# Attention beside a state-space scan on one core: another order ahead of the first exp, and a new plan

## The chip, the cores and the metric

The kernel runs on one core of a Trainium2 chip. Its time is the device time of one execution in microseconds (us); of several executions the median counts, and lower is better. Five engines work side by side, each through its own queue in order: TensorE (PE; PEld is its weight load), VectorE (DVE), ScalarE (ACT), GpSimd (POOL) and SyncE (SP), which issues most of the DMAs. They meet through semaphores.

## What is computed

Two independent layers on sequences of 2048 rows of 640 bf16 numbers; their outputs are laid side by side.

```python
# A: a diagonal state space layer
Lam_bar = jnp.exp(dt * Lam);  B_bar = ((Lam_bar - 1.0) / Lam)[:, None] * Bmat
Bu = jnp.einsum("bld,pd->blp", x + 0j, B_bar)
for t in range(L): h = Lam_bar[None, :] * h + Bu[:, t, :]
y = 2.0 * jnp.einsum("blp,dp->bld", hseq, Cmat).real + x * Dskip
# B: attention, 32 query heads of 20 numbers, one key head and one value head
q = (x @ wq).reshape(B, S, 32, 20);  k = x @ wk;  v = x @ wv
p = softmax(einsum("bhqd,bkd->bhqk", q, k) * 20 ** -0.5)
o = einsum("bhqk,bkd->bhqd", p, v) ... @ wo
```

## The kernel before

Softmax dominates: 2048 tiles of 128 keys by 512 queries need an exponential. The kernel takes no exact row maximum but a bound: the key maximum times the sum of a query's absolute values. That bound enters as one more row of the queries (QT), so scores come out of TensorE ready for the exponential.

Tiles go two ways. ScalarE reads two or three of them at once out of a **slot** (two slots SC0 and SC1 of three PSUM banks each) and writes bf16 weights PR. VectorE takes other tiles, mostly from the third bank of a slot, and makes an approximate exponential by writing the bits of a bf16 number; it and GpSimd then add constants to make three shifted copies in BIG, and TensorE sums all four with scaled values VS. A fill of a slot with scores is one step on TensorE, since scores use 32 of its 128 rows each; a piece of other work, such as a query product, may **ride** on the free rows. Everything else, the scan of layer A, query products and output products, is fitted between.

The order of all of this is no loop. The program hands steps (`pe`, `dve`, `act`, `pool`, `dma`) with estimated durations, dependencies and priorities to a planner (`Schedule`) that plays them through; `Emitter` writes each engine's queue in the order found and puts in the semaphore waits. Seeds (`SEEDS`) shift the background work, and the table `STAGES` gives the planner's weights from a given tile count on. `LANDS` and `XB` say when it expects the first loads. None of these numbers are in the program that runs, only the order that they lead to.

What comes ahead of the first exp:

- `loads`: x for layer B comes in four blocks of 512 rows. Blocks 0 and 1 are loaded plain (xn, into CT) and turned by TensorE against an identity (L730, `turn`), then copied out (L1139 on VectorE, L1142 on ScalarE); blocks 2 and 3 come by transposing DMA (L715). The key weights wk are spread four times over the columns (`wks_op`, L1047, on ScalarE). The first 80 columns of wq (`wqa`) are padded by GpSimd (L1069) for the first query product.
- `kv_steps`: per block five products make the keys, spread over four groups of partitions (L1162); VectorE reduces their absolute maximum (L1168, into mab); the keys are scaled into KT on ScalarE (L1174) or VectorE (by the helper `ts`, L867), as `KEYS` says. Values (L1218) follow and are copied to VP (L1226) and, scaled, to VS.
- `bound`: one reduction over the five maxima (L1194) and the mask times the result, M0 (L866).
- `qt_task`: the first query product (L1279) goes to QT on ScalarE (L1292), its absolute values (L866) are multiplied by M0 on TensorE (L730, four matmuls 32x512), and VectorE writes the final QT (L867).
- `ssm_scalars`: the scan's tables `tab` by sine on ScalarE from the angles `fr`, of which VectorE makes five and GpSimd (L2215) five more.
- TensorE runs products of zeros (L730 MATMUL MB<-PR) where it would idle here.
- `attention`: when all six banks of the slots are free (`mine`), fills (L1626) and exps (L1530) begin. The third bank of each slot is lent to background work until the first query load is ordered.

Names that are not tensors: `prio` orders steps that could start at the same time (lower first), `gate` holds a step back in the plan, `port` marks the SBUF port that VectorE and GpSimd share. L800, L810 and L730 are helpers of TensorE, L862, L866 and L867 of VectorE, L710, L711 and L715 of loads.

Of the kernel before, what the change touches and what calls it, by code (L numbers as in the profile page):

```python
# [11 lines left out]
ACT = mybir.ActivationFunctionType  # L12
ALU = mybir.AluOpType
# [454 lines left out]
class Build:  # L468
# [79 lines left out]
    SEEDS, REPLAYS = (169732,), 12  # L548
# [321 lines left out]
    def program(self):  # L870
        self.lay_banks()
        self.firsts, self.row_mm, self.stage_dma, self.buf_user, self.unit_due = [], {}, {}, {}, {}
        self.tile_n = 0
# [156 lines left out]
    def loads(self):  # L1030
# [24 lines left out]
        self.vec_op.append(vec[3]("sp"))  # L1055
        self.wqa_op = L(wqd[:, :, 0:80], wqv[:, :, 0:80], 200000, "wqa", strided=True, writes=["wqa"], prio=0)
# [31 lines left out]
    PLAIN, KP, QR, FRP, SINP, SKIP_P, KEY_BANKS = 2, (1.04, 1.04, 1.06, 1.08), 1.05, 0.34, 0.32, 1.03, "2543016"  # L1088
    WKP, QUAD_KEYS, WKE = 0.9, 0, "a"
    TURNED, KEYS = ("adada", "adada"), "adaa"  # L1090
    XB = ((2, 0, 5, 11250.0), (3, 0, 3, 12500.0), (3, 3, 5, 13400.0))
    LANDS = (2250.0, 2400.0, 2750.0, 8200.0, 5600.0, 7900.0, 6500.0, 8450.0, 14600.0, 17000.0)
# [35 lines left out]
    def kv_steps(self):  # L1128
# [20 lines left out]
        def kv(tb):  # L1149
# [4 lines left out]
            steps = [(0, c, 512) for c in range(NC)] if tb < 3 else self.KEY_STEPS  # L1154
            for x, c, n in steps:
                at = 512 * tb + n * x
# [10 lines left out]
                if c == NC - 1:  # L1167
                    red = self.dve(lambda e, src=bank.cols(n * x, n * x + n), to=p.mab[:, tb + x:tb + x + 1]: e.tensor_reduce(  # L1168
                        out=to, in_=src, axis=AX.X, op=ALU.max, apply_absolute_value=True), 115 + 1.05 * n, deps=[prev], reads=[bank.key],
                        writes=[f"mab{tb + x}"], prio=0.31 if tb < 3 or x else 0.315)  # L1170
                    self.red_op[tb + x] = red
# [20 lines left out]
        def bound():  # L1192
            yield lambda: len(self.red_op) == 5
            m = self.dve(lambda e: e.tensor_reduce(out=p.mab[:, 5:6], in_=p.mab[:, 0:5], axis=AX.X, op=ALU.max), 120,  # L1194
                         deps=list(self.red_op.values()), reads=[f"mab{i}" for i in range(5)], writes=["mabs"], prio=0.3)
            self.m0_op = self.dve(self.ts(p.M0[:], p.mask0[:], p.mab[:, 5:6], None, ALU.mult), 200, port=True,
                                  deps=[m, self.c_op["mask0"]], reads=["mabs", "mask0"], writes=["M0"], prio=0.3)
# [529 lines left out]
    SCARCE = 8  # L1727
# [945 lines left out]
```

## Time and profile before

| | us |
|---|---|
| median of 3 executions (697.73 to 699.15) | 698.69 |
| the profiled execution, its own time | 697.62 |
| its span, first to last instruction | 695.9 |
| busy in the span: PE, ACT, DVE, POOL | 683.2, 681.8, 637.0, 470.4 |
| first exp starts | 18.41 |
| last exp ends | 687.68 |

Two engines are busy for 98% of the span, so busy shares tell little here. The granted TensorE clock is 1.00 throughout. What is of use is the view by stages (ahead of the first exp, the exps, the end), the pace of the exps in the timeline, and the chain of waits of the first stage. Note that ScalarE's entries overlap: an exp's time in the groups is longer than the distance from its start to the next one's.

### The profile page before, as it was taken

What the parts mean: (1) busy time and instruction counts of PE and PEld (TensorE: products, weight loads), DVE (VectorE), ACT (ScalarE), POOL (GpSimd) and SP (SyncE); (2) the same over time, 40 slices, a digit from 0 to 9 for tenths busy, and PEclk for the clock granted to TensorE, in tenths of its full rate; (3) what the DMA queues carried; (4) which work ended last, traced back from release to release, by engine and by line L of the source; (5) the groups of instructions that cost most, each with busy time, mean ns of one, the idle gap of its engine ahead of it and who ended that gap; (6) DMA issues with size and microseconds to landing.
All of it is one profiled execution on the core that took longest, in us unless ns stands there. A gap on an engine that the chain in (4) does not pass through costs nothing.

```text
span 695.9 us, 27390 instructions
## 1 busy us (share of the span) xinstructions
PE 683.2 (98%) x11488; PEld 250.6 (36%) x11490; DVE 637.0 (92%) x1243; ACT 681.8 (98%) x703; POOL 470.4 (68%) x796
## 2 busy tenths in 40 slices
PE   8999999999999999999999999999999999999998
PEld 5322332334334333333433333334333332343335
DVE  7899999999999889999999999999999999977795
ACT  7999999999999999999999999999999999999996
POOL 4256666564587668767778777676776767788880
DMA  9659641211130111102110101131000001110001
GB/s 217 175 127 187 139 103 39 62 26 32 30 94 13 32 27 27 35 21 29 44 26 22 28 27 28 35 58 20 13 15 12 20 15 36 37 29 22 21 15 41
DMA packets 77591, 34.48 MB, mean 50 GB/s; under 512 B 58350, under 2 KB 77470, under 8 KB 77470
## 3 DMA queue, kind: packets, MB, share of 16 engines
q1 hardware_dynamic: 76650, 32.57, 20.3%
q8 instruction: 92, 1.51, 0.9%
q10 hardware_dynamic: 820, 0.16, 0.1%
q14 instruction: 29, 0.24, 0.1%
HBM read 11.53 MB, written 9.75 MB: 31 GB/s over the span
## 4 chain that ended last, share of the span: by engine, by line
PE 56%; ACT 42%; DVE 1%; issue 0%
ACT PR L1530 41%; PE MB L1946 21%; PE MB L800 14%; PE SC L1626 10%; PE MB L810 8%; PE MB L730 1%; DVE BIG L867 1%; PE SC L1162 1%; PE SC L726 1%; PE MB L726 0%; ACT L2197 0%; PE SC L730 0%; DVE pvsb L1925 0%; PE MB L1279 0%; DVE QT L867 0%
## 5 line engine op out<-in xcount | busy, mean ns | idle before, releaser
L1530 ACT ACTIVATE PR<-SC 128x1024 bf16<-128x1024 f32 (+1 forms) x678 | 666.6, 1131 | 4.5 <-PE SC L1626 3.3
L1858 POOL INT64_ADD BIG<-BIG x761 | 458.1, 617 | 198.1 <-DVE BIG L867 54.7
L867 DVE TENSOR_SCALAR BIG<-SC 128x512 int16<-128x512 f32 x560 | 376.2, 684 | 38.7 <-PE SC L1626 33.1
L1946 PE MATMUL MB<-BIG,VS 128*32 128x512 bf16 (+1 forms) x2468 | 269.8, 376 | 1.2 <-DVE pvsb L1925 0.9
L1626 PE MATMUL SC<-QT,KT 32*128 32x512 bf16 (+1 forms) x2073 | 265.3, 378 | 4.4 <-ACT PR L1530 1.8
L1946 PE MATMUL MB<-PR,VP 128*32 128x512 bf16 (+1 forms) x1495 | 222.3, 378 | 0.1
L1626 PEld LDWEIGHTS SC<-QT,KT 32*128 32x128 bf16 x2073 | 67.3, 91 | 133.8 <-ACT PR L1530 77.1
L1946 PEld LDWEIGHTS MB<-BIG,VS 128*32 128x32 bf16 x2468 | 68.5, 95 | 65.5 <-issue 41.4
L1946 PEld LDWEIGHTS MB<-PR,VP 128*32 128x32 bf16 x1495 | 55.1, 94 | 45.8 <-issue 33.0
L867 DVE TENSOR_SCALAR BIG<-BIG 128x1024 int16<-128x1024 int16 (+1 forms) x136 | 52.3, 419 | 0.9 <-PE MB L1946 0.4
L800 PE MATMUL MB<-CA,W 128*32 128x320 bf16 (+2 forms) x992 | 51.4, 299 | 0.4 <-DVE BIG L2366 0.4
L810 PE MATMUL MB<-xaT,BT 32*128 32x256 bf16 x192 | 37.1, 273 | 0.0
L800 PE MATMUL MB<-CT,W 128*32 128x512 bf16 (+1 forms) x640 | 36.0, 302 | 0.6 <-issue 0.6
L800 PE MATMUL MB<-xaT,BA 128*32 128x256 bf16 x800 | 31.8, 275 | 0.0
L810 PE MATMUL MB<-diagD,xaT 32*128 32x128 bf16 x320 | 31.3, 217 | 0.0
L810 PEld LDWEIGHTS MB<-diagD,xaT 32*128 32x128 bf16 x320 | 17.7, 92 | 29.1 <-ACT PR L1530 17.7
L800 PEld LDWEIGHTS MB<-CA,W 128*32 128x32 bf16 x992 | 22.8, 96 | 14.2 <-issue 5.7
L800 PE MATMUL MB<-xaT,BT 128*32 128x256 bf16 x608 | 26.2, 274 | 0.0
L2133 DVE CAST stg<-MB 128x512 bf16<-128x512 f32 x35 | 23.8, 680 | 1.8 <-PE MB L800 1.1
L862 DVE TENSOR_TENSOR prod<-MB,tab 128x1024 bf16<-128x1024 f32 x20 | 24.3, 1215 | 0.2
L867 DVE TENSOR_SCALAR BIG<-MB 128x512 int16<-128x512 f32 x35 | 23.8, 679 | 0.6 <-PE MB L1626 0.6
L2406 DVE TENSOR_TENSOR_SCAN g<-sc,hst,prod 128x256 bf16<-128x256 f32 x30 | 22.5, 749 | 0.0
(178 smaller groups left out, 502.4 us busy)
## 6 DMA issues: line engine op xcount, KB each, us to landing
out_dram<-stg SPq DMA_DIRECT2D x33, 128.0 KB, 2.0
qd<-BIG SPq DMA_DIRECT2D x20, 128.0 KB, 2.1
QT<-qd SPq DMA_DIRECT2D x28, 80.0 KB
OP<-pvsb SPq DMA_DIRECT2D x105, 20.0 KB
rdP<-recs SPq DMA_DIRECT2D x105, 20.0 KB
lbd<-BA SPq DMA_DIRECT2D x5, 320.0 KB, 2.7
CT<-in_B_x_dram SPq DMA_DIRECT2D x2, 640.0 KB, 5.3
BA<-in_A_B_re_dram SPq DMA_DIRECT2D x1, 800.0 KB, 7.5
```

Source lines behind the costliest of these rows:

```text
L726: r = e.matmul(out[32 * j:32 * j + 32], lhsT=lhsT[:, 32 * j:32 * j + 32], rhs=rhs, start=start, stop=stop, tile_position=(0, 32 * j), skip ...
L730: return lambda e: e.matmul(out, lhsT=lhsT, rhs=rhs, start=start, stop=stop, **kw)
L800: x = e.matmul(out[32 * j:32 * j + 32], lhsT=lhsT[:, 32 * j:32 * j + 32], rhs=rhs, start=start, stop=r.end is tag, tile_position=(0, 32 * ...
L810: return lambda e: e.matmul(out, lhsT=lhsT[at], rhs=rhs[at], start=start, stop=r.end is tag, tile_position=(32 * row, 0), skip_group_check ...
L862: return lambda e: e.tensor_tensor(out, a, b, op)
L867: return lambda e: e.tensor_scalar(out, a, s1, s2, op0=op0, op1=op1)
L1530: ex = self.act(lambda e: e.activation(dst, t[:, 0:512 * n], ACT.Exp, scale=1.0 / UNIT), 0.8333 * 512 * n + 64, table="exp", deps=[op], re ...
L1626: r = e.matmul(out[:, bank.off + lo:bank.off + lo + n], lhsT=p.KT[32 * j:32 * j + 32, 128 * c:128 * c + 128], rhs=p.QT[32 * j:32 * j + 32, ...
L1858: op.fns.append(lambda e: e.int64_add(words(dst), words(src), add))
L1946: r = e.matmul(bank.tensor[32 * j:32 * j + 32, bank.off + at:bank.off + at + n], lhsT=v[:, c, 0:32], rhs=rhs[:, lo:lo + n], start=first an ...
L2133: ev = self.dve(lambda e: e.tensor_copy(st, bank.ap), 645, deps=[prev], reads=[bank.key], writes=[key], prio=self.EV, gate=(lambda: last.e ...
L2406: o = self.dve(lambda e, ri=ri, init=init: e.tensor_tensor_scan(p.g[:, u, ri, :], rdec, p.prod[:, 1, 0, ri, :], init, ALU.mult, ALU.add), ...
```

## The change

Ahead of the first exp:

1. VectorE spreads the key weights, and is to do so early (`prio=0.2`); GpSimd's angles wait for it in the plan.
2. The first wq columns and the Dskip row are issued from ScalarE's queue.
3. The keys of block 1 are scaled on VectorE, not ScalarE.
4. Block 3's keys are made in five products of 512, no longer in halves, and reduced once. The key maximum comes in two steps: the maximum of blocks 0 to 2 times the mask on ScalarE, and then, on VectorE, one instruction that takes in block 3's. The value for all blocks that the rest needs is reduced behind it.
5. The first fill waits for two banks of each slot only, so not for those of the values.

In the attention: a fill may leave out its third bank, and the wait for VectorE's reading of it, when the plan sees that reading come too late (`third_late`); such a fill holds two tiles. And the planner has another seed, other weights and other expected landings, so the order changes everywhere.

```diff
-    SEEDS, REPLAYS = (169732,), 12
+    SEEDS, REPLAYS = (696354,), 12
...
             self.wks_op = self.dve(lambda e: e.tensor_copy(spread, again), 400, deps=[self.wk_op], reads=["wkr"], writes=["wks"],
-                                   prio=0.34, port=True)
+                                   prio=0.2, port=True)
...
-        self.vec_op.append(vec[3]("sp"))
-        self.wqa_op = L(wqd[:, :, 0:80], wqv[:, :, 0:80], 200000, "wqa", strided=True, writes=["wqa"], prio=0)
+        self.wqa_op = L(wqd[:, :, 0:80], wqv[:, :, 0:80], 200000, "wqa", eng="act", strided=True, writes=["wqa"], prio=0)
+        self.vec_op.append(vec[3]("act"))
...
-    WKP, QUAD_KEYS, WKE = 0.9, 0, "a"
-    TURNED, KEYS = ("adada", "adada"), "adaa"
+    WKP, QUAD_KEYS, WKE = 0.9, 0, "d"
+    TURNED, KEYS = ("adada", "adada"), "ddaa"
...
-            steps = [(0, c, 512) for c in range(NC)] if tb < 3 else self.KEY_STEPS
-            for x, c, n in steps:
-                at = 512 * tb + n * x
+            x, n, at = 0, 512, 512 * tb
+            for c in range(NC):
...
-            yield lambda: len(self.red_op) == 5
-            m = self.dve(lambda e: e.tensor_reduce(out=p.mab[:, 5:6], in_=p.mab[:, 0:5], axis=AX.X, op=ALU.max), 120,
-                         deps=list(self.red_op.values()), reads=[f"mab{i}" for i in range(5)], writes=["mabs"], prio=0.3)
-            self.m0_op = self.dve(self.ts(p.M0[:], p.mask0[:], p.mab[:, 5:6], None, ALU.mult), 200, port=True,
-                                  deps=[m, self.c_op["mask0"]], reads=["mabs", "mask0"], writes=["M0"], prio=0.3)
+            yield lambda: all(i in self.red_op for i in range(3))
+            m = self.dve(lambda e: e.tensor_reduce(out=p.mab[:, 4:5], in_=p.mab[:, 0:3], axis=AX.X, op=ALU.max), 120,
+                         deps=[self.red_op[i] for i in range(3)], reads=[f"mab{i}" for i in range(3)], writes=["mab4"], prio=0.3)
+            m = self.act(lambda e: e.activation(p.M0[:].rearrange("p a b -> p (a b)"), p.mask0[:].rearrange("p a b -> p (a b)"), ACT.Copy,
+                                                scale=p.mab[:, 4:5]), 260,
+                         deps=[m, self.c_op["mask0"]], reads=["mab4", "mask0"], writes=["M0"], prio=0.25)
+            yield lambda: 3 in self.red_op
+            self.m0_op = self.dve(lambda e: e.scalar_tensor_tensor(out=p.M0[:], in0=p.mask0[:], scalar=p.mab[:, 3:4], in1=p.M0[:],
+                                                                   op0=ALU.mult, op1=ALU.min), 250, port=True,
+                                  deps=[m, self.red_op[3]], reads=["mab3", "mask0", "M0"], writes=["M0"], prio=0.3)
...
-        mine = [b for _, bs in self.slots for b in bs]
+        mine = [b for _, bs in self.slots for b in bs[:-1]]
...
-            yield lambda: (fill is None or fill.start is not None) and all(o.start is not None
-                                                                          for o in self.slot_last[i])
+            yield lambda: (fill is None or fill.start is not None) and all(o.start is not None for o in self.slot_last[i] if o is not self.third[i]) \
+                and self.third_known(i)
...
-            deps = list(self.slot_last[i])
+            self.skip[i] = self.third_late(i)
+            deps = [o for o in self.slot_last[i] if o is not self.third[i] or not self.skip[i]]
...
     STAGES = (
         (0, {'STAY': 1.2, 'PAUSE': 500.0, 'pe': 192.807, 'dve': 150.0, 'KEEP_C': 3, 'OPEN': 1, 'PATIENCE': 2500.0, 'MARGIN':
-            648.138, 'WAITING': 2, 'REFILL': 905.623, 'SPARE': 148.045, 'LAG': 162.255, 'SOON': 3981.867, 'EARLIER': 3, 'LATER':
...
+            569.99, 'WAITING': 3, 'REFILL': 905.623, 'SPARE': 148.045, 'LAG': 162.255, 'SOON': 224.375, 'EARLIER': 3, 'LATER': 3,
...
+    def third_late(self, i):
+
+        o = self.third[i]
+        return o is not None and (o.start is None or self.s.seen(o, "pe") > max(self.third_limit(i), self.s.t))
...
+        if self.skip[i]:
+            n, third = min(n, 2), self.third[i]
+            self.n_skip += 1
```

What this does to the queues, at three places. SP's queue, from its first loads on; in the old order:

```order
L711 DMA vrow<-in_A_Lambda_re_dram 5x128
L711 DMA CT<-in_B_x_dram 128x4x640 x2
L711 DMA vrow<-in_A_Dskip_dram 5x128
L710 DMA BIG<-in_B_wq_dram 128x5x80
L715 DMA_TRANSPOSE BIG<-in_B_x_dram 128x5x512
L715 DMA_TRANSPOSE BIG<-in_B_x_dram 128x3x512
```

and in the new one:

```order
L711 DMA vrow<-in_A_Lambda_re_dram 5x128
L711 DMA CT<-in_B_x_dram 128x4x640 x2
L715 DMA_TRANSPOSE BIG<-in_B_x_dram 128x5x512
L715 DMA_TRANSPOSE BIG<-in_B_x_dram 128x3x512
L715 DMA_TRANSPOSE BIG<-in_B_x_dram 128x2x512
```

The Dskip row and the 80 columns of wq are gone from it; they stand behind wk in ScalarE's queue, ahead of its first table load.

VectorE's queue from the last maximum but one to QT (mab are the maxima; MB2 is the bank of the first query product), in the old order:

```order
L1168 TENSOR_REDUCE mab<-SC0 128x1
L866 TENSOR_SCALAR BIG<-QT 128x512
L1168 TENSOR_REDUCE mab<-SC1 128x1 x2
L1194 TENSOR_REDUCE mab<-mab 128x1
L866 TENSOR_SCALAR M0<-mask0,mab 128x128
L867 TENSOR_SCALAR QT<-MB2,lift 128x512
```

and in the new one, from one row earlier:

```order
L866 TENSOR_SCALAR BIG<-QT 128x512
L1167 TENSOR_REDUCE mab<-SC0 128x1
L985 MEMSET VS 128x16
L1193 TENSOR_REDUCE mab<-mab 128x1
L1167 TENSOR_REDUCE mab<-SC1 128x1
L1199 SCALAR_TENSOR_TENSOR M0<-mask0,mab,M0 128x128
L1202 TENSOR_REDUCE mab<-mab 128x1
L867 TENSOR_SCALAR QT<-MB2,lift 128x512
```

Behind the last block's reduction there stands one instruction where there were two, and a reduction over few numbers has moved ahead of it.

TensorE's queue from the last keys to the first fill (SC1 is the slot in which block 3's keys and the values are made, wvr are the value weights, the bracket names what a row waits for), in the old order:

```order
L1162 MATMUL SC1<-BIG,wks 128x256 x3
L730 MATMUL MB3<-PR 128x512
L1218 MATMUL SC1<-wvr,BIG 128x20 [waits dma_wv]
L1218 MATMUL SC1<-wvr,BIG 128x20 x19
L730 MATMUL MB3<-PR 128x512 x2
L730 MATMUL MB2<-BIG,M0 32x512 [waits prog_dve]
L730 MATMUL MB2<-BIG,M0 32x512 x3
L1218 MATMUL SC1<-wvr,BIG 128x20 [waits prog_act]
L1218 MATMUL SC1<-wvr,BIG 128x20 x19
L730 MATMUL MB3<-PR 128x512 x2
L810 MATMUL SC0<-BIG 128x512 [waits dma_wq,prog_act,prog_dve]
L1626 MATMUL SC0<-QT,KT 128x512 x2
```

and in the new one:

```order
L1161 MATMUL SC1<-BIG,wks 128x512 [waits dma_xb33]
L1161 MATMUL SC1<-BIG,wks 128x512
L1224 MATMUL SC1<-wvr,BIG 128x20 [waits dma_wv,prog_dve]
L1224 MATMUL SC1<-wvr,BIG 128x20 x39
L730 MATMUL MB3<-PR 128x512
L730 MATMUL MB2<-BIG,M0 32x512 [waits prog_dve]
L730 MATMUL MB2<-BIG,M0 32x512 x3
L730 MATMUL MB3<-PR 128x512 x4
L810 MATMUL SC0<-BIG 128x512 [waits dma_wq,prog_act,prog_dve]
L1661 MATMUL SC0<-QT,KT 128x512 x2
```

The values of two blocks now stand together ahead of the product with M0; the first fill has a rider (L810) that waits for the load of wq, as before.

More of the change, by code (lines that the diff above doesn't have):

```diff
@@ L1307, in qt_task @@
         self.give(bank)
-    m0_op = None
+    m0_op = q_first = None
     row_mm = {}
@@ L1408, in attention @@
             self.misc.append(lent)
-            self.free_banks.append(lent)
+            if not lent.busy:
+                self.free_banks.append(lent)
         s.spawn(self.reclaim())
@@ new lines, in third_limit, with third_known @@
+    def third_limit(self, i):
+        ex, other = self.slot_last[i][0], self.slot_last[1 - i][0]
+        return ex.start + ex.dur + (other.dur if other.eng == "act" else 0.0) - 522.0 + self.SKIP
+    def third_known(self, i):
+        o = self.third[i]
+        if o is None or o.start is not None:
+            return True
+        at = self.third_limit(i) - 755.0
+        if self.s.t < at:
+            self.s.at(at)
+            return False
+        return True
+    def third_late(self, i):
+        o = self.third[i]
+        return o is not None and (o.start is None or self.s.seen(o, "pe") > max(self.third_limit(i), self.s.t))
@@ L1539, in fill @@
         ex.hook = on_start
-        self.slot_last[i] = [ex] + first
+        self.slot_last[i] = [ex] + first + ([third] if third is not None else [])
+        self.third[i] = first[0] if first else third
         for (b, kc, j, rhs), key in zip(ents, keys):
@@ L1815 @@
     BACKLOG = 9
-    LAST = 12
-    POOL_LAST = 14
+    LAST = 14
+    POOL_LAST = 27
     def pool_source(self):
```

77 lines of the change are left out of this document (41 added, 36 removed).

## The prediction, made before the changed kernel had run

> **What bounds the kernel now.** I read the stages first: busy time of each engine before the first exp, between the first exp's start and the last one's end, and behind it.
>
> ```profile
> core 0: us, PE busy (x) PEld busy (x) DVE busy (x) ACT busy (x) POOL busy (x), PEclk, DMA share, GB/s
> 0.00:18.41 18.41, 16.02 (x134) 9.09 (x136) 13.83 (x56) 13.03 (x21) 8.14 (x27) 1.00 0.92 225
> 18.41:687.68 669.27, 661.87 (x11232) 238.45 (x11234) 621.28 (x1184) 666.61 (x678) 462.26 (x769) 1.00 0.19 44
> 687.68:695.90 8.22, 5.29 (x131) 3.10 (x125) 1.92 (x4) 2.17 (x4) 0.00 (x0) 1.00 0.28 82
> ```
>
> In the middle stretch ScalarE stands still for 669.27 - 666.61 = 2.66 us. The length is therefore 18.41 us until ScalarE may begin its 678 exps, the exps themselves, and 8.22 us of end. Next, the groups by form and the exps at their own pace:
>
> ```profile
> L1530 ACT ACTIVATE PR<-SC 128x1024 bf16<-128x1024 f32 x579 | 544.7, 1068 | 4.3 <-PE SC L1626 3.3 <-PE MB L1626 0.3 <-PE MB L1946 0.2
> L1530 ACT ACTIVATE PR<-SC 128x1536 bf16<-128x1536 f32 x98 | 141.6, 1505 | 0.1
> ...
> 511.75 8.38 ACT L1530 ACTIVATE PR<-SC 128x1024 bf16<-128x1024 f32 x9
> 518.08 2.06 ACT L1530 ACTIVATE PR<-SC 128x1024 bf16<-128x1024 f32 x2
> ...
> 683.06 4.13 ACT L1530 ACTIVATE PR<-SC 128x1536 bf16<-128x1536 f32 x3
> 685.72 1.47 ACT L1530 ACTIVATE PR<-SC 128x1536 bf16<-128x1536 f32 x1
> ```
>
> Consecutive exps overlap, so the mean of one (1068 ns) is not what one costs. From start to start a fed two-bank exp takes (518.08 - 511.75) / 7 = 0.904 us, a three-bank exp (685.72 - 683.06) / 2 = 1.33 us. At that pace, with the one exp of a single bank at half a two-bank one, the stretch would be 579 x 0.904 + 98 x 1.33 + 0.45 = 654.2 us; it is 669.3. So 15 us are lost, 2.66 of them as visible standstill, the rest in short delays that hide in the overlap. For those I look at what TensorE's weight loads for scores waited for:
>
> ```profile
> PEld SC L1626 <- DVE BIG L867: 31.3, 77, 0.7
> ```
>
> The columns are us in total, times, longest: 31.3 us of it ends with VectorE emptying a slot's third bank. Last, the chain of waits up to the first exp:
>
> ```profile
> 7.30 0.63 ACT wks L1047
> ...
> 7.98 0.61 PE SC L1162 x2
> ...
> 11.64 1.08 PE MB L1279 x5
> ...
> 15.10 0.66 PE SC L1218 x20
> ...
> 16.25 0.43 PE MB L730 x4
> ...
> 16.70 0.81 DVE QT L867
> 17.51 0.29 DVE VP L1226 x2
> ...
> 17.98 0.37 PE SC L810
> ```
>
> It runs from the spread key weights (L1047) through TensorE's keys, the first query product (L1279) and the value products (L1218) to the key maximum's product (L730), QT, and two value copies (L1226) that the scores wait for.
>
> **The change, part by part.** *Key weights on VectorE.* The chain leaves ScalarE at 7.93. In the new order VectorE makes three `fr` steps, one cast, then `wks`. The fr group and the cast group (rows below) give a start near 7.29: three fr steps at 1.41 / 5 end near 6.7, and a cast is followed after about 0.6 (two in 1.28). For the copy of 128x640 bf16 the trace has ends: 0.22 (VectorE's pass over 128x256 bf16 at 24.76) and 0.72 (the same copy on ScalarE, L1047). I take 0.38, nearer the VectorE row: TensorE starts at 7.7, 0.25 earlier; bounds 0.4 earlier to 0.1 later.
>
> ```profile
> 5.89 1.41 DVE L867 TENSOR_SCALAR fr<-iota,trig 128x256 int32<-128x256 f32 x5
> 7.21 1.28 DVE L1139 CAST BIG<-SC 128x512 bf16<-128x512 f32 x2
> 24.76 0.22 DVE L866 TENSOR_SCALAR tab<-tab 128x256 bf16<-128x256 bf16 x1
> ```
>
> The Trainium skill (VectorE: DVE Perf Modes, "The perf-mode tier table") lets a bf16 SBUF copy run at four elements a cycle; with the 150 fixed cycles that the page measured that is an estimate of (150 + 160) / 0.96 = 0.32 us, which would move the chain by another 0.06 us. No row here has this copy.
>
> *Two loads leave SP's queue.* SP issues the Dskip row (0.48 us) and the first columns of wq (0.38 us) ahead of the transposing loads of x; now ScalarE does.
>
> ```profile
> 2.26 0.48 SPq L711 DMA_DIRECT2D vrow<-in_A_Dskip_dram  x1
> 2.79 0.38 SPq L710 DMA_DIRECT2D BIG<-in_B_wq_dram  x1
> 3.21 8.38 SPq L715 DMA_TRANSPOSE BIG<-in_B_x_dram  x3
> 11.64 0.59 SPq L710 DMA_DIRECT2D wvr<-in_B_wv_dram  x1
> 12.27 0.52 SPq L710 DMA_DIRECT2D BIG<-in_B_wq_dram  x1
> ...
> BIG<-in_B_wq_dram SPq DMA_DIRECT2D x1, 700.0 KB, 5.6
> wkr<-in_B_wk_dram ACTq DMA_DIRECT2D x1, 25.0 KB, 4.9
> wvr<-in_B_wv_dram SPq DMA_DIRECT2D x1, 25.0 KB, 3.4
> ...
> 4.55 0.21 ACT L2190 ACTIVATE sc<-sc 128x5 f32<-128x5 f32 x1 [1.05 <-DVE sc L2178]
> 8.87 0.52 POOL L1069 COPY wqp<-BIG 128x400 bf16<-128x400 bf16 x1
> ```
>
> The transposing loads may start 3.21 - 2.26 = 0.95 us earlier, and with them the value weights (issued at 11.64, landing at 15.0) and the rest of wq (issued 12.27, landing about 17.85). The DMA engines are busy meanwhile (share 0.92), so the bytes compete: 0 to 0.95 us, I take the middle, 0.45. On ScalarE the two issues (0.86 us) push its first table load back; behind that load it now idles 1.05 us, until 4.55, so they are covered with 0.19 us to spare. The wq columns feed POOL's copy for the first query product, which TensorE reaches at 11.6; behind wk (issue to landing 4.9) they have until about 11.
>
> The Trainium skill (DMA: Bandwidth & Descriptors, "Issuing engines are not separate DMA queues") says loads from any queue share the same 16 engines and a second issuing engine saves sequencer time alone. By that rule the landings would not move, wq would hold the first score until 17.9, and the head would gain 0.1 us instead of 0.45; the DMA share of 0.92 is on its side.
>
> *Maximum in two steps.* Now, from TensorE's last key:
>
> ```profile
> 12.29 0.74 DVE L867 TENSOR_SCALAR KT<-SC,lift 128x512 bf16<-128x512 f32 x1
> ...
> 13.84 0.69 DVE L1168 TENSOR_REDUCE mab<-SC 128x1 f32<-128x512 f32 x1
> 14.92 0.76 DVE L1168 TENSOR_REDUCE mab<-SC 128x1 f32<-128x256 f32 x2 [0.19 <-PE SC L1162]
> 15.71 0.16 DVE L1194 TENSOR_REDUCE mab<-mab 128x1 f32<-128x5 f32 x1
> 15.91 0.29 DVE L866 TENSOR_SCALAR M<-mask,mab 128x128 bf16<-128x128 f32 x1
> ```
>
> Two half reductions, a small one and the mask: 14.92 to 16.20. After: one reduction (0.69) and one combined step, which I put at the mask's 0.29 (nothing nearer; 0.2 to 0.4): 14.92 to 15.94. Against the 0.26 saved stand the 0.74 us of a second key copy on VectorE and the first maximum's 0.16, which leave VectorE free for the last reduction only about 0.1 later: 0.12 saved. ScalarE's part (128x128) fits in between. All 40 value matmuls now stand ahead of the maximum's product, and 20 take up to 0.66 us: with weights at 15.0 TensorE would be free only at about 16.3, with my 0.45 at about 15.9. Both then agree on about 15.9, against 16.25 now.
>
> *Scores without the values' banks.* QT then ends near 17.2, and the 0.47 us from 17.51 to 17.98 fall to the usual 0.1. What is late next is wq: the first fill carries a piece of a query product as a rider, so it waits for that load, 17.85 - 0.45 = 17.4. First score 17.5, first exp 17.95: the head is 0.45 us shorter (0 to 0.95).
>
> *The new plan.* It holds 572 two-bank and 104 three-bank exps: 572 x 0.904 + 104 x 1.33 = 655.4 us, 1.2 us more at full pace, since VectorE gives three tiles back. VectorE's work falls:
>
> ```profile
> L867 DVE TENSOR_SCALAR BIG<-SC 128x512 int16<-128x512 f32 x560 | 376.2, 684 | 38.7 <-PE SC L1626 33.1
> L867 DVE TENSOR_SCALAR BIG<-BIG 128x1024 int16<-128x1024 int16 x127 | 50.2, 427 | 0.9 <-PE MB L1946 0.4
> ```
>
> Six of the first (-4.1 us) and ten of the second (-4.3) go, three of about 0.68 come from other banks (+2.0): 6.4 us less. TensorE's streamed columns stay the same within 1 us. The skip of a late third bank is new, but the order shows it idle: all 18 fills of two tiles without a VectorE tile (19 before) are among the first 26. So what may shrink is the delay, by the freed VectorE time. Bounds: the visible 2.66 us gone, or every 50 us as bad as the worst one:
>
> ```profile
> 318.41:368.41 50.00, 49.33 (x53) 1.00 0.18 35
> ```
>
> 13.4 x 0.67 - 2.66 = +6.3 us. I take -2.4, nearer the first end, because VectorE, on which 31.3 us of the fills' waiting hangs, has less to do. The end (same products, same four last evacuations) I leave at 0, within 0.4.
>
> Sum: -0.45 + 1.2 - 2.4 = -1.65 us against the profiled execution's 697.62 us (span 695.9 and 1.7 around it): 695.97. The median of the runs lies 1.07 above, so 698.69 - 1.65 = **697.0 us**. A measurement of this kernel tells about 0.2%, 1.4 us.
>
> **Rivals.** *Delays unchanged.* The new rule fires nowhere, so the plan is as good as before: -0.45 + 1.2 = +0.75, 699.4. For it: the counts; against: the freed VectorE time.
> *The loads land no earlier.* Then the head gives 0.1 and the forecast's sum is -1.3: 697.4. For it: DMA share 0.92; against: two issues less on SP.
> *Slower: fills wait more for VectorE's third bank.* In TensorE's queue a fill that waits holds all behind it, and ScalarE drains. At 0.4 us each (31.3 us in 77 waits) it decides from about two more waits on top of +0.75 (over 700.1); six more give 698.69 + 0.75 + 2.4 = 701.8. For it: 31.3 us of such waiting, and a plan whose drain times are estimates; against: VectorE's load falls.
> *Slower: the wq columns come late in ScalarE's queue.* If behind wk they took its 4.9 us once more, they would land past 11.4, POOL's copy (0.52) would end at 12 and TensorE would stand 0.5 us, which eats the head's gain: 698.69 + 1.2 + 0.5 = 700.4 with delays unchanged.
>
> **How the numbers follow.** Forecast 0.46; delays unchanged 0.20; loads unmoved 0.10; third bank 0.17; late wq columns 0.07. Faster 0.46, same 0.30, slower 0.24. The forecast's own range is 695.0 to 697.3 (head 0.95, and 1.5 more of the hidden delay); the whole range goes up into the third-bank case, with four of its six waits: 695.0 to 701.0.
>
> **What would show it.** First exp near 17.95, ended by TensorE's rider product and the wq load; `wks` on VectorE under 0.5 us; TensorE gapless from 7.7; ScalarE's standstill in the exps' stretch near 0.4 us. A standstill of 2.7 us or more, or a first exp past 18.4, makes the forecast wrong.

## The result and the profile after

The changed kernel takes 701.18 us (median of 6, 700.31 to 701.87) against 697.89 us (6 executions beside it, 696.45 to 699.15): ratio 1.0045, 95% interval 1.0032 to 1.0059. It is 0.45% slower; 697.0 had been forecast. The profiled executions differ alike: spans 699.4 and 695.9.

The stages of the changed kernel, cut like those of before (ahead of the first exp, the exps, the end):

```profile
core 0: us, PE busy (x) PEld busy (x) DVE busy (x) ACT busy (x) POOL busy (x), PEclk, DMA share, GB/s
0.00:18.86 18.86, 16.38 (x134) 8.92 (x134) 14.46 (x57) 12.28 (x20) 8.17 (x27) 1.00 0.93 231
18.86:691.04 672.18, 661.20 (x11187) 238.51 (x11187) 617.75 (x1165) 669.29 (x676) 464.70 (x777) 1.00 0.18 44
691.04:699.40 8.36, 5.25 (x136) 2.69 (x134) 2.43 (x6) 2.17 (x4) 0.00 (x0) 0.94 0.29 82
```

The head is 0.45 us longer (18.41 before), not 0.45 shorter; the exps' stretch 2.9 us longer (669.27); the end 0.14. VectorE's busy time in the stretch fell by 3.5 us (621.28 to 617.75), and the stretch grew all the same. The exps by form:

```profile
L1564 ACT ACTIVATE PR<-SC 128x1024 bf16<-128x1024 f32 x572 | 539.2, 1068 | 5.0 <-PE SC L1661 4.1
...
L1564 ACT ACTIVATE PR<-SC 128x1536 bf16<-128x1536 f32 x104 | 149.3, 1503 | 0.1
```

572 and 104 are the forecast's counts, and the mean times (1068, 1503 ns) are those of before: 655.4 us at full pace, 1.2 more. The rest, 672.2 - 655.4 = 16.8 against 15.1, is 1.7 us more delay.

**The head.** ScalarE's queue in the timeline, then SP's and VectorE's row for the key weights:

```profile
2.21 0.54 ACTq L710 DMA_DIRECT2D BIG<-in_B_wq_dram  x1
2.79 0.74 ACTq L711 DMA_DIRECT2D vrow<-in_A_Dskip_dram  x1
3.56 1.28 ACT L2225 ACT_TABLE_LOAD   x1 [3.56 <-DVE vsc L985]
4.85 0.21 ACT L2225 ACTIVATE sc<-sc 128x5 f32<-128x5 f32 x1
```

```profile
2.27 9.67 SPq L715 DMA_TRANSPOSE BIG<-in_B_x_dram  x3
11.98 0.58 SPq L710 DMA_DIRECT2D wvr<-in_B_wv_dram  x1
12.61 0.52 SPq L710 DMA_DIRECT2D BIG<-in_B_wq_dram  x1
```

```profile
7.58 0.47 DVE L1050 COPY wks<-wkr 128x640 bf16<-128x640 bf16 x1
```

The two issues push the table load from 2.22 to 3.56, which is 1.34 and not 0.86, and its first use from 4.55 to 4.85. So VectorE's angles, and the key weights behind them, come 0.3 us later than reckoned (7.58, not 7.29). SP's transposing loads start 0.94 earlier (3.21 before) and yet need 9.67 us instead of 8.38, so wv and wq are issued 0.34 later than before, not earlier. TensorE from the last keys to the first fill:

```profile
15.79 1.16 PE L1224 MATMUL SC<-wvr,BIG 128*128 128x20 bf16 x40 [0.59 <-DMA wvr<-in_B_wv_dram]
16.80 0.38 PE L730 MATMUL MB<-PR 128*128 128x512 bf16 x1
17.10 0.40 PE L730 MATMUL MB<-BIG,M 128*32 128x512 bf16 x4
17.44 1.04 PE L730 MATMUL MB<-PR 128*128 128x512 bf16 x4
18.43 0.39 PE L810 MATMUL SC<-BIG 32*128 32x512 bf16 x1
```

M0 is ready at 16.39 (L1199, 16.04 plus 0.35), but its product begins at 17.10, behind 40 value products that waited for wv. QT ends at 18.37, and the first score begins at 18.43.

**The delays.** I took, for each exp, the time from the start of the one ahead less 0.904 or 1.33 us. The four longest delays are now 0.97 (exp at 626.0), 0.73 (79.7), 0.63 (231.2) and 0.61 (478.3), in all 2.95; before, 0.83, 0.54, 0.50 and 0.36, in all 2.23. What TensorE waited for ahead of three of them, and where VectorE stood then:

```profile
78.40 0.40 PE L1981 MATMUL MB<-BIG,VS 128*32 128x512 bf16 x3 [0.53 <-POOL BIG L1893]
...
477.88 0.23 PE L810 MATMUL MB<-diagD,xaT 32*128 32x128 bf16 x1 [0.61 <-issue]
...
625.32 0.24 PE L800 MATMUL MB<-CT,W 128*32 128x128 bf16 x3 [0.68 <-issue]
```

```profile
76.97 0.55 DVE L867 TENSOR_SCALAR W<-CT,sc 128x1280 bf16<-128x1280 bf16 x1 [0.99 <-DMA CT<-in_A_C_im_dram]
```

None of the four ends with a third bank. At 77 VectorE stood 0.99 us at the head of its queue for a load; in the chain of waits GpSimd's next addition begins right behind that scaling (77.69), and TensorE stood 0.53 us for the addition. The two "issue" rows are standstills in which TensorE waited for nothing that the profile names. Such standstills of over 0.15 us last 1.5 us in all here and 1.0 in the profile of before; the delays of the two exps behind each sum to 2.4 and 1.4.

Sorted by size, however, the long delays are not what came on top:

| sum of delays, us (number) | under 0.1 | 0.1 to 0.2 | 0.2 to 0.3 | over 0.3 |
|---|---|---|---|---|
| before | 7.2 | 2.4 (20) | 1.8 (7) | 3.5 (8) |
| b_loads (order of before, see below) | 7.4 | 2.9 (23) | 1.5 (6) | 4.4 (8) |
| changed | 7.3 | 4.4 (33) | 1.5 (6) | 3.3 (5) |
| its 8 variants below | 7.3 to 8.1 | 4.1 to 5.0 (30 to 37) | 1.3 to 1.7 | 2.2 to 4.2 |

The delays of 0.1 to 0.2 us grew, by 2.0 us, and are as large in every profile of the new order. In all 20 of them before and in 31 of the 33 after, the exp starts some 0.05 us behind the last score of its fill, and TensorE's row has no gap in the 1.5 us ahead. The slot had been free for some time: its last exp had ended 0.2 to 1.0 us before the fill began, and VectorE's last reading of a bank over 0.2 us before it in all but one case before and two after. So TensorE came late to these fills, from other products, and not because it waited for ScalarE or VectorE.

### The profile page after: what moved, and what is told of

It is laid out like the page before. It is cut to its first block, busy times and chain, and to the rows that moved or that the text cites. A ratio compares the mean times of both kernels' runs of the same rounds, so it can differ in the third digit from the quotient of the medians.

```text
span 699.4 us, 27266 instructions
## 1 busy us (share of the span) xinstructions
PE 682.8 (98%) x11451; PEld 250.1 (36%) x11451; DVE 634.6 (91%) x1227; ACT 683.7 (98%) x700; POOL 472.9 (68%) x804
## 4 chain that ended last, share of the span: by engine, by line
ACT 50%; PE 41%; DVE 4%; DMA 3%; SPq 1%; issue 1%; ACTq 0%; POOL 0%; DVEq 0%; POOLq 0%
ACT PR L1564 49%; PE MB L1981 15%; PE MB L800 10%; PE SC L1661 8%; PE MB L810 5%; DVE BIG L867 2%; DMA mrep<-mab 1%; DMA CT<-in_A_C_im_dram 1%; SPq L715 1%; PE SC L1161 1%; PE SC L726 1%; PE MB L726 0%; DMA mcol<-mrep 0%; PE MB L730 0%; DVE BIG L1324 0%
## 5 line engine op out<-in xcount | busy, mean ns | idle before, releaser
L1564 ACT ACTIVATE PR<-SC 128x1024 bf16<-128x1024 f32 (+1 forms) x676 | 669.3, 1135 | 5.1 <-PE SC L1661 4.1
L867 DVE TENSOR_SCALAR BIG<-SC 128x512 int16<-128x512 f32 x554 | 371.6, 683 | 43.9 <-PE SC L1661 37.8
L1981 PE MATMUL MB<-PR,VP 128*32 128x512 bf16 (+1 forms) x1502 | 216.5, 378 | 0.0
L867 DVE TENSOR_SCALAR BIG<-BIG 128x1024 int16<-128x1024 int16 (+1 forms) x121 | 48.3, 428 | 2.4 <-PE MB L1981 2.0
L810 PE MATMUL MB<-xaT,BT 32*128 32x256 bf16 x192 | 37.2, 273 | 0.0
L810 PE MATMUL MB<-diagD,xaT 32*128 32x128 bf16 x320 | 31.4, 217 | 0.6 <-issue 0.6
L810 PEld LDWEIGHTS MB<-diagD,xaT 32*128 32x128 bf16 x320 | 17.7, 92 | 29.4 <-ACT PR L1564 18.3
L867 DVE TENSOR_SCALAR BIG<-MB 128x512 int16<-128x512 f32 x38 | 25.8, 679 | 0.1
L800 PE MATMUL MB<-BIG 128*32 128x512 bf16 x296 | 22.9, 383 | 0.0
```

The source lines that it names most:

```text
L800: x = e.matmul(out[32 * j:32 * j + 32], lhsT=lhsT[:, 32 * j:32 * j + 32], rhs=rhs, start=start, stop=r.end is tag, tile_position=(0, 32 * ...
L810: return lambda e: e.matmul(out, lhsT=lhsT[at], rhs=rhs[at], start=start, stop=r.end is tag, tile_position=(32 * row, 0), skip_group_check ...
L867: return lambda e: e.tensor_scalar(out, a, s1, s2, op0=op0, op1=op1)
L1564: ex = self.act(lambda e: e.activation(dst, t[:, 0:512 * n], ACT.Exp, scale=1.0 / UNIT), 0.8333 * 512 * n + 64, table="exp", deps=[op], re ...
L1981: r = e.matmul(bank.tensor[32 * j:32 * j + 32, bank.off + at:bank.off + at + n], lhsT=v[:, c, 0:32], rhs=rhs[:, lo:lo + n], start=first an ...
```

## The experiments

So that an edit doesn't change the whole order, most kernels let the planner run as it is, then move a few steps in the list that it made. All other rows of the queues stay word for word.

```diff
-                plan.s.run()
+                plan.s.run(); moved(plan, plan.s.order)
```

**Which queue issues the two loads.** Once back to SP in the changed kernel (a_loads), once to ScalarE in the kernel before (b_loads):

```diff
+    two = [self.vec_op[3], self.wqa_op]              # a_loads
+    for o in two: order.remove(o); o.eng = "sp"
+    at = order.index(self.xb_op[2, 0]); order[at:at] = two
+    two = [self.wqa_op, self.vec_op[3]]              # b_loads
+    for o in two: order.remove(o); o.eng = "act"
+    at = order.index(self.wk_op) + 1; order[at:at] = two
```

> The changed kernel, order kept, but the Dskip row and the first wq columns are issued from SP's queue ahead of the transposing loads, as before the change. Theory L (the loads' move delays): the three transposing loads of x land at 11.25, 13.05, 14.2 again (11.57, 13.36, 14.55 in the changed kernel), wv at 15.05 (15.65), ScalarE's first table load starts at 2.2 (3.56) and the keys start at 7.8 to 8.0 (8.11); value products end near 16.3, the product with M0 begins near 16.5 (17.10), first exp 18.3 to 18.4, held by wq at 17.85. Rival E (as the prediction had it, SP's two issues are what the loads wait for): the loads land 0.4 to 0.9 later than in the changed kernel, first exp 19.2 or later.

> The kernel before, order kept, but the first wq columns and the Dskip row are issued from ScalarE's queue behind wk: this one part of the change alone. Theory L: SP's first transposing load is issued 0.95 earlier, and yet x's blocks and wv land 0.3 to 0.6 later than in the kernel before (11.25, 13.04, 14.22; wv 15.05), ScalarE's first table load starts 1.3 later and its chain through wks 0.3 later: first exp 18.55 to 18.75 instead of 18.41. Theory E (prediction): x's blocks and wv land 0.45 (0 to 0.95) earlier: first exp 18.4 or earlier.

Ratios to the kernel before: a_loads 1.0047 (1.0030 to 1.0064), b_loads 1.0012 (1.0002 to 1.0021). All heads stand in one table (landings as the trace has them, in us):

| kernel | issued by | last x | wv | wq | M0 product | QT ends | first score | first exp |
|---|---|---|---|---|---|---|---|---|
| before | SP | 14.22 | 15.05 | 17.84 | 16.25 | 17.51 | 17.98 | 18.41 |
| b_loads | ScalarE | 14.83 | 15.10 | 17.95 | 16.85 | 18.11 | 18.23 | 18.66 |
| changed | ScalarE | 14.55 | 15.65 | 17.85 | 17.10 | 18.37 | 18.43 | 18.86 |
| a_loads | SP | 14.52 | 15.43 | 18.55 | 16.88 | 18.15 | 18.69 | 19.12 |
| a_m0b | ScalarE | 14.45 | 15.24 | 18.26 | 16.35 | 17.61 | 18.40 | 18.83 |
| a_headb | SP | 14.42 | 15.30 | 18.49 | 16.32 | 17.59 | 18.63 | 19.06 |
| a_wq | SP | 14.11 | 17.45 | 17.11 | 16.01 | 17.28 | 17.34 | 17.77 |

b_loads did what theory L said: first exp at 18.66, 0.25 later, with x later by 0.3 to 0.6 though its loads were issued 0.94 earlier (wv, however, only 0.05 later). a_loads fits neither theory: ScalarE's chain went back as L said,

```profile
2.24 1.28 ACT L2225 ACT_TABLE_LOAD   x1 [2.24 <-DVE one L985]
4.55 0.21 ACT L2225 ACTIVATE sc<-sc 128x5 f32<-128x5 f32 x1 [1.03 <-DVE sc L2213]
```

but x landed no earlier than in the changed kernel, wq 0.7 later, and the first exp came at 19.12. One execution's landings scatter by several tenths, so a single pair doesn't decide the sign. Over all profiles of this case the last x block landed at 14.11 to 14.52 with the two loads in SP's queue (7 profiles, median 14.34) and at 14.27 to 14.88 with them in ScalarE's (8, median 14.55): by the medians the move makes x later by some 0.2, not earlier.

**Where the values stand.** a_m0 and a_head put the product with M0 ahead of block 1's values, and with that ahead of the step that brings block 3's maximum into M0; that part of the computation is left out in them. a_m0b and a_headb put block 1's values behind the product instead. The two with "head" also have the loads in SP's queue.

```diff
+    m = self.row_mm[-1]                              # a_m0b: the product with M0
+    vals = [o for o in order[:order.index(m)] if o.eng == "pe" and "wvr" in o.reads]
+    zeros = [o for o in order[order.index(vals[0]):] if o.eng == "pe" and o.reads == ["PR0"]]
+    for o in vals[2:] + zeros[:3]: order.remove(o)
+    order[order.index(vals[0]):order.index(vals[0])] = zeros[:2]
+    order[order.index(m) + 1:order.index(m) + 1] = vals[2:]
```

> The changed kernel, order kept word for word but for TensorE's head: the product with M0 stands ahead of the values of block 1, two products of zeros ahead of the values of block 0, one product of zeros is left out. Theory Q (queue place): M0 was made at 16.39 but its product began at 17.10, behind 40 value products that waited for wv (landing 15.65); so the product now begins at 16.4 to 16.5, QT ends at 17.75, and the load of wq (17.85) is what the first score waits for: first score 17.95, first exp 18.35 to 18.4, 0.5 us earlier than 18.87. Rival F (floor): 40 value products (1.16 us) have to run ahead of the first fill anyway, and moving one past them gains nothing: first exp 18.8 to 18.9. Behind the first exp nothing changes under either.

> Both edits at once: loads back in SP's queue, the product with M0 ahead of block 1's values. Theory W (wq is the floor): the product with M0 begins near 16.1, QT ends near 17.0, but the first fill carries a piece of a query product that waits for wq (17.85), so the first exp comes at 18.3, no earlier than either edit alone. Rival S (QT is what counts): first exp 0.06 + 0.44 us behind QT's end, so 17.5 to 17.6.

> The changed kernel, order kept but for TensorE's head: the values of block 1 (20 products) stand behind the product with M0, two products of zeros ahead of the values of block 0, one product of zeros is left out. (In a_m0 and a_head the product with M0 was taken before block 3's maximum had entered M0; here it waits for it.) Theory Q (queue place): the product with M0 begins at 16.45 to 16.6 instead of 17.10, QT ends near 17.8, wq's load (17.6 to 17.9) and QT bind together: first exp 18.35 to 18.45. Rival F (floor): the 20 products behind it hold the first fill, first exp 18.8 to 18.9.

> Loads back in SP's queue and the values of block 1 behind the product with M0. wks starts near 7.3 (7.58 in the changed kernel), M0 is made at 16.0 to 16.2, its product begins at 16.1 to 16.3, QT ends near 17.1 to 17.4. Theory W (wq is the floor): first score only when wq has landed (17.8), first exp 18.3 to 18.4. Rival S: first exp half a us behind QT's end, 17.6 to 17.9.

a_m0 and a_head: first exp at 18.39 and 18.36, as theories Q and W said, with QT's end at 17.90 and 17.49 and wq at 17.62 and 17.79. a_m0b's timeline of TensorE:

```profile
16.35 0.40 PE L730 MATMUL MB<-BIG,M 128*32 128x512 bf16 x4 [0.33 <-DVE M L1199]
16.68 0.66 PE L1224 MATMUL SC<-wvr,BIG 128*128 128x20 bf16 x20
17.20 0.59 PE L730 MATMUL MB<-PR 128*128 128x512 bf16 x2
18.39 0.37 PE L810 MATMUL SC<-BIG 32*128 32x512 bf16 x1 [0.60 <-DMA BIG<-in_B_wq_dram]
```

The product now begins as soon as M0 is there and QT ends at 17.61, 0.76 earlier: theory Q's place was right. The first exp is not earlier, because TensorE stands 0.60 us for wq, which landed at 18.26. a_headb shows the same (QT 17.59, wq 18.49, first score 18.63), against rival S. In every row of the table the first score begins 0.06 to 0.14 behind the later of QT's end and wq's landing. (Ratios: a_m0 1.0080, a_head 1.0048, a_m0b 1.0048, a_headb 1.0078, the last from 1.0052 to 1.0105.)

**wq ahead of wv.** The decisive test, with SP's queue as in a_loads. Since wv now lands later, the value products move behind the second fill:

```diff
+    order.remove(self.wq_op); order.insert(order.index(self.wv_op), self.wq_op)
...
+    late = [o for o in order[:order.index(m)] if o.eng == "pe" and "wvr" in o.reads] + [self.vp_op[0], self.vp_op[1], self.vs_op[0], self.vs_op[1]]
...
+    order[order.index(fills[1]) + 1:order.index(fills[1]) + 1] = late
```

> The changed kernel with the two loads back in SP's queue, wq's load issued ahead of wv's, and the value products of blocks 0 and 1 (with VectorE's copies of them) behind the second fill; the rest of the order is kept. wq's load is issued 0.63 earlier. Theory W (wq is the floor): M0 is made near 16.2, its product begins at 16.3, QT ends near 17.55; wq lands 17.2 to 17.6, so the first score starts 0.06 to 0.15 behind the later of the two, at 17.65 to 17.75, and the first exp at 18.1 to 18.2, 0.7 us earlier than in the changed kernel; the exps right behind it may be late, since the values now stand between fills. Rival B (the bytes decide, not the place in the queue): wq lands at 17.8 or later whatever its place, first exp 18.35 or later. The total moves by less than the measurement tells.

The chain of waits of a_wq:

```profile
15.61 0.36 DVE M L1199
15.97 0.04 issue
16.01 1.37 PE MB L730 x8
17.38 0.34 PE SC L810
17.72 0.22 PE SC L1661 x4
17.93 1.10 PE SC L1224 x40
```

wq lands at 17.11, now ahead of QT's end at 17.28, and the first score begins at 17.34, the first exp at 17.77: 1.09 us ahead of the changed kernel and 0.64 ahead of the kernel before, more than expected because x came early too. So wq was the floor of the first exp, and with it gone QT is. But nothing was saved. The second and third exp came late behind the values, as the exps in the timeline show:

```profile
19.35 1.02 ACT L1564 ACTIVATE PR<-SC 128x1024 bf16<-128x1024 f32 x1 [0.56 <-DVE VP L1232]
20.73 5.70 ACT L1564 ACTIVATE PR<-SC 128x1024 bf16<-128x1024 f32 x6 [0.35 <-PE SC L1661]
```

These two were 0.67 and 0.47 us late, and the eighth exp starts at 25.39, against 25.34 in the changed kernel and 24.81 in the kernel before. The span is still 699.4: the stretch is 672.57, the end 9.08. The ratio is 1.0064 (1.0045 to 1.0083).

**The plan.** Seeds and tables exchanged between the two kernels, and the next seed in each:

```diff
-    SEEDS, REPLAYS = (169732,), 12                   # before_s2
+    SEEDS, REPLAYS = (169733,), 12
-    SEEDS, REPLAYS = (696354,), 12                   # after_s2
+    SEEDS, REPLAYS = (696355,), 12
+    # after_oldplan: SEEDS, STAGES, LAST, POOL_LAST, EARLY_*, FIRST_P, C_*, CB_*, Q_*, O_*, SSM_* of before
+    # before_newplan: the same names, of the changed kernel
```

> The changed kernel with the old numbers of the plan: seed, STAGES, LAST, POOL_LAST and the due times of the background work as before the change; the edits ahead of the first exp stay. It holds 569 two-bank and 109 three-bank exps: 569 x 0.904 + 109 x 1.33 = 659.3 us at full pace (before 654.2, after 655.4). Theory P (the length of the exps' stretch is the full pace of the counts plus 15 to 18 us of delays): stretch 674.5 to 677.5, time about 704. Rival C (counts do not decide: VectorE, with fewer tiles, delays less): stretch 669 to 673. Rival H (the edits ahead of the first exp lengthen the stretch, not the numbers): stretch at the changed kernel's 672.

> The kernel before with the new numbers of the plan (seed, STAGES, LAST, POOL_LAST, due times); nothing else of the change. 566 two-bank and 108 three-bank exps: 655.3 us at full pace. Theory P: stretch 655.3 + 15 to 18 = 670 to 673, head 18.4 or so. Rival H: stretch near the 669.3 of before, at most 670, since the edits ahead of the first exp are not in it.

> The kernel before with the next seed (169733), nothing else. 571 two-bank and 104 three-bank exps: 654.5 us at full pace. Theory P, and that plans scatter: stretch 654.5 + 15 to 18 = 669.5 to 672.5, though no line of the program changed: a difference of 1 to 3 us by the draw of the order alone. Rival N (the order's draw matters little): within 0.7 us of 669.3.

> The changed kernel with the next seed (696355), nothing else. 557 two-bank, 117 three-bank exps and one of a single bank: 659.6 us at full pace, 4.2 more than the changed kernel. Theory P: stretch 674.5 to 677.5, 2.5 to 5 us longer than the changed kernel's 672.2. Rival C: within 1 us of 672.2.

The middle and end of before_s2 and after_s2 in the view by stages:

```profile
18.71:691.34 672.63, 663.09 (x11200) 241.38 (x11202) 624.08 (x1198) 668.25 (x675) 451.50 (x752) 1.00 0.19 44
691.34:700.16 8.82, 5.32 (x152) 2.71 (x140) 2.52 (x5) 2.18 (x5) 0.00 (x0) 0.95 0.27 79
```

```profile
18.62:692.68 674.06, 663.16 (x11190) 239.29 (x11192) 611.91 (x1155) 671.95 (x676) 458.42 (x764) 1.00 0.19 44
692.68:701.98 9.30, 5.78 (x141) 3.77 (x132) 2.46 (x7) 2.73 (x6) 0.00 (x0) 0.97 0.24 72
```

| kernel | two-, three-bank exps | full pace | stretch | delays | end | ratio of times to before |
|---|---|---|---|---|---|---|
| before | 579, 98 | 654.2 | 669.3 | 15.1 | 8.2 | |
| b_loads (same order) | 579, 98 | 654.2 | 670.5 | 16.3 | 7.9 | 1.0012 |
| changed | 572, 104 | 655.4 | 672.2 | 16.8 | 8.4 | 1.0045 |
| its 8 variants a_... | 572, 104 | 655.4 | 671.6 to 673.3 | 16.2 to 17.9 | 8.1 to 9.2 | 1.0037 to 1.0080 |
| before_s2 | 571, 104 | 654.5 | 672.6 | 18.1 | 8.8 | 1.0055 (1.0038 to 1.0071) |
| before_newplan | 566, 108 | 655.3 | 673.7 | 18.4 | 15.3 | 1.0145 (1.0126 to 1.0165) |
| after_oldplan | 569, 109 | 659.3 | 675.4 | 16.1 | 13.2 | 1.0171 (1.0154 to 1.0189) |
| after_s2 | 557, 117 | 659.6 | 674.1 | 14.5 | 9.3 | 1.0083 (1.0067 to 1.0099) |

Another seed, with no line of the program changed, makes the kernel before 0.55% slower and its stretch 3.4 us longer: no less than the whole change did. Theory P held for the size: stretches follow the counts plus 14.5 to 18.4 us of delay (after_s2 0.4 under its range, before_s2 and before_newplan 0.1 and 0.7 over). Rival H fell: before_newplan has none of the edits ahead of the first exp, and its stretch is longer than the changed kernel's. Rival C fell in its strong form, since 3.9 and 4.2 us more of full pace than the changed kernel's cost 3.2 and 1.9; delays were smaller in after_s2 (14.5), but not much in after_oldplan (16.1). The numbers of one kernel cost 5 to 7 us in the end stage of the other: in before_newplan VectorE stood there 3.7 us for a store.

```profile
704.30 0.69 DVE L2135 CAST stg<-MB 128x512 bf16<-128x512 f32 x1 [3.71 <-DMA out_dram<-stg]
```

The new skip of a late third bank plays no part: with `third_late` made to return False, the changed kernel's queues are row for row the same on all five engines (from the order alone, no run).

**VectorE at the head of its queue.**

```diff
+    o = self.c_scaled[0]; order.remove(o)            # a_w: W<-CT three instructions later
+    order.insert(order.index(self.c_scaled[1]), o)
```

> The changed kernel, order kept, but VectorE's first scaling of C (W<-CT, which stood 0.99 us for the load of C's imaginary part at 76) comes three instructions later, behind brow, a copy and a third-bank evacuation. Theory V (VectorE's queue head on a DMA): the copy and POOL's add are early enough, TensorE's 0.53 us wait for POOL at 78.4 and the 0.73 us delay of the exp at 79.7 go; other delays stay: the exps' stretch is 0.5 to 0.8 us shorter. Rival P (TensorE or POOL is late there for another reason): the exp near 79.7 is still delayed by 0.4 us or more.

The delay at 79.7 was gone, the stretch 672.40, not shorter by 0.5 to 0.8 as theory V had it (ratio 1.0043, 1.0026 to 1.0059). But the delay was gone as well in all seven other variants, without that edit, and a_w stood 0.97 us for another load at 96; a_loads stood 1.42 us at 103.6 and lost 1.69:

```profile
103.61 0.29 DVE L866 TENSOR_SCALAR BIG<-BIG 128x512 int16<-128x512 int16 x1 [1.42 <-DMA qd<-BIG]
```

So VectorE does stand for loads and exps are late behind it, but the place changes from execution to execution, and a_w can't tell what the edit did.

**TensorE's standstills without a cause.**

```diff
+    for k, n in ((47, 2), (51, 1), (55, 4), (56, 1), (122, 3), (135, 3), (168, 1), (178, 1), (179, 2), (186, 1), (192, 2), (353, 1)):
+        fns = [self.mm(bank.tensor[32 * j:32 * j + 32, bank.off:bank.off + 16], self.VZ[:], self.KT[:, 0:16], False, False,
+                       tile_position=(0, 32 * j), skip_group_check=True) for j in range(4)] * n
...
+        order.insert(order.index(fills[k]), o)
```

> The changed kernel, order kept, with 176 more TensorE instructions (22 groups of four tiny products of zeros, 32x16, and their weight loads) placed before exp 360 where TensorE waits for ScalarE anyway; they add zero. TensorE's code comes in pieces of 16 KB, about 256 instructions, by the queue of instructions (92 pieces), and the standstills with no visible cause at 477.9 (0.61) and 625.3 (0.68) end 2.65 and 2.45 us after a piece's transfer began. Theory C (code loading): the pieces now end 176 instructions earlier in the program, so these two standstills change: each by over 0.3 us, shorter or gone, or new ones at another place; every standstill of over 0.3 us without a cause ends 2.2 to 2.7 us behind the start of a piece. Rival D (the place itself, such as those products' operands): standstills of 0.5 to 0.7 us at the same two exps (459 and 610).

Ratio 1.0037 (1.0023 to 1.0051). The pieces of code did start about 176 instructions earlier in the program, and the standstills moved with them: the delayed exps are 460 and 611 instead of 459 and 610, ahead of other products, and a new one of 0.81 came at 228.

```profile
626.50 0.27 PE L800 MATMUL MB<-BIG,xaT 128*32 128x128 bf16 x5 [0.81 <-issue]
```

```profile
227.97 0.22 PE L800 MATMUL MB<-CA,W 128*32 128x128 bf16 x1 [0.81 <-issue]
```

Rival D fell. One of the two changed by 0.26 and the other by 0.13, less than the 0.3 written down, and one ended 2.75 us behind its piece, just past the window.

The place in the program settles it. Number TensorE's instructions (weight loads, products, semaphores) by their start: the product that ends such a standstill (over 0.15 us, "issue") is number 191 to 195 behind a multiple of 256 in all 44 cases that the 15 profiles of this case have. In the changed kernel the two are numbers 15,811 and 20,674, in a_fetch 16,066 and 20,929: 255 further on where 176 were put in, so 79 instructions later in the program, at the same place of a piece.

## Why the prediction was wrong

The forecast's sum was -1.65 us; the profiles differ by +3.5. Of these 5.1 us, 0.9 lie in the head, 4.1 in the delays of the exps and 0.1 in the end. So the term of -2.4 for the delays failed most, and the -0.45 for the head came out with the other sign.

- **Two loads leave SP's queue (-0.45 taken): the step that failed first.** The prediction charged the loads with waiting for SP's issues. With the DMA engines at a share of 0.93 in this stage, loads issued earlier took longer (9.67 against 8.38 us of issuing, and b_loads' landings). wq landed at 17.85, against 17.4 forecast and 17.84 before. The rule weighed there (the Trainium skill, DMA: Bandwidth & Descriptors, "Issuing engines are not separate DMA queues": other queues save sequencer time alone) gave 17.9; the trace agrees, and x even came later.
- **ScalarE's two issues:** 0.86 taken, 1.34 measured, against a cover of 1.05. The 0.3 us left over delayed the angles and the key weights.
- **Key weights on VectorE:** right in kind. 0.47 us against 0.38 taken (by the Trainium skill, VectorE: DVE Perf Modes, "The perf-mode tier table", the estimate was 0.32; the trace is above it), and a start at 7.29 exactly as forecast in a_head, a_headb and a_wq, where the loads stay in SP's queue (7.41 in a_loads); 7.58 in the changed kernel.
- **Maximum in two steps:** the combined step took 0.35 (0.29 taken). But "both agree on about 15.9" rested on wv at 14.6. It landed at 15.65, and 40 products ahead of M0's made the latter 0.85 later than before. a_m0b shows this term alone.
- **Scores without the values' banks:** the 0.47 us put down to the value copies were wq's. Before, the first score began 0.14 behind wq's landing (17.84), just as in a_m0b (0.14) and a_headb (0.14). In b_loads, with the old wait, the two copies ended at 18.26 and 18.41 and the first score began at 18.22, ahead of both. The wait that was removed cost nothing.
- **The new plan (+1.2 at full pace, -2.4 of delay taken): the step that failed most.** The counts came out. The delay went up 1.7 instead, and the variants of the same order lie 1 to 3 us above the 15.1 of before. The -2.4 rested on TensorE's 31.3 us of waits for VectorE's third bank, as if the exps paid for them. They pay little of it:

```profile
PEld SC L1661 <- DVE BIG L867: 34.9, 84, 0.9
```

  The waits even grew (31.3 us in 77 before), though VectorE did 3.5 us less in the stretch (6.4 forecast); yet the exps that start next behind such a wait were late by 2.4 us in all before and 2.2 after. What grew are the delays of 0.1 to 0.2 us (2.4 to 4.4 us), where TensorE, which the prediction took as unchanged, is at other products until the fill is late. Why the new order has more such places is open. TensorE's standstills behind code and VectorE's waits for loads make the longest delays, but their sum is that of the execution: b_loads, in the order of before, lost 2.2 us behind such standstills.
- By its own signs the forecast was wrong: ScalarE's standstill is 672.18 - 669.29 = 2.89 us (0.4 expected, 2.7 the limit), and the first exp is past 18.4.
- **The rivals:** "loads unmoved" was right on the landings. "Third bank" has nearly the right time (701.8), and the waits that it counts did grow by seven, but the exps behind them were no later than before, so its mechanism isn't where the time went here; in before_s2 (99 waits) those exps were late by 5.6 us. The late wq columns didn't come late (9.03, needed by about 11).

What stays open: the executions of the changed kernel's variants scatter over 2 to 5 us (a_wq 701.04 to 705.31), those of the kernel before measured beside a_wq no less (696.98 to 702.28), and none of the longest was profiled. VectorE's waits for DMAs, 0.4 to 1.4 us in places that change, are a candidate, not shown; the longest of all (707.16, of a_headb) had a granted clock of 0.993, but others nearly as long had 1.00 (704.57, of a_w). It is also open whether the 0.64 us that a_wq's first exp gains on the kernel before can be kept; no version here beats that kernel.

## What to carry to other kernels

Before giving a time to a wait that is removed, look for the second latest thing at that place and put its landing beside it; here a load landed 0.14 us before the step that seemed to wait for copies. Before giving a price to a sum of waits, see how late the work behind them was: 31.3 us of waits stood for 2.4 us of late exps. Where the DMA engines were at 0.9 of a stage, an earlier issue bought nothing, and the order of the loads counted: with wq ahead of wv the first exp came 0.64 us ahead of the kernel before. But follow such a gain past the first exp: by the eighth it was gone. And where a planner reorders everything, measure what another seed does first: 3.4 us of stretch here, more than any edit of the head brought.

## What the runs showed of the hardware

TensorE can stand still while its code is loaded. The page's row of the queue for instructions in the changed kernel:

```profile
q8 instruction: 92, 1.51, 0.9%
```

92 pieces of 16 KB for some 23,500 instructions of TensorE are one for about 256. Half of these pieces last TensorE 7.9 us or more; the 256 instructions ahead of a standstill were gone in 2.5 to 5.5 us (median 3.4), mostly where short products follow one another (128x128 in groups of four). In the 15 profiles of this case, all 44 standstills of TensorE in the stretch of over 0.15 us that end with "issue" end 2.16 to 2.92 us behind the start of such a piece's transfer, up to 1.02 us long, and all at the same place of a piece (191 to 195 behind a multiple of 256). The Trainium skill (Runtime: NRT & Kernel Launch, "Instruction fetch mechanics") says that blocks of 256 instructions are fetched ahead and that crossing a boundary is mostly hidden; here it is hidden in most of the 92 cases, and the delays behind the rest sum to 1.4 us before and 2.4 us after.

Also, two issues from ScalarE's queue took 0.54 and 0.74 us where SP had needed 0.38 and 0.48 for the same loads.
